# Turning by VectorE in 32 by 32 blocks instead of by TensorE: routed attention followed by a mixture of experts

## The chip, the cores and the metric

The kernel runs on one core of one Trainium2 chip. The metric is the device time of one execution in microseconds (us), here the median of three runs. The core has five engines that run side by side, each with its own queue of instructions, worked off in order: TensorE (PE) multiplies matrices and can also turn (transpose) a tile by multiplying it with an identity matrix; VectorE (DVE) and ScalarE (ACT) work element by element[...], and SyncE (SP) issues transfers. TensorE writes into the small memory PSUM[...]; the large memory on the core is SBUF, with 128 partitions (rows).

## The reference, cut to what matters

Attention among tokens of the same cluster, then a mixture of eight experts in which each token goes to one expert.

```python
# q, k, v: (4 batches, 8 heads, 768 positions, 64 dims); centroids: (8 heads, 16 clusters, 64 dims)
q_assign = np.argmax(np.einsum('bhsd,hcd->bhsc', q_n, c_n), axis=-1)   # nearest centroid of each query
k_assign = np.argmax(np.einsum('bhsd,hcd->bhsc', k_n, c_n), axis=-1)
mask = q_assign[:, :, :, None] == k_assign[:, :, None, :]
scores = scale * np.matmul(q, k.transpose(0, 1, 3, 2))                 # scale = 1 / sqrt(64)
scores = np.where(mask, scores, -1000000000.0)
attn = softmax(scores)                                                 # written out in the reference
x = np.matmul(attn, v)                                                 # to (3072 tokens, 512)
# experts: y = relu(x_e @ w1[e]) @ w2[e] for the tokens of expert e, times the gate's weight
```

## The kernel before

Heads are worked two at a time: a *pair* g is one batch and two heads, and there are NG = 16 pairs. A pair has 12 *score units* (2 halves of the queries by 6 blocks of 128 keys), done in 2 *turns* of 6 units (NB = 6, TG = 2). The even turn 2g does the first half of the queries, the odd turn 2g+1 the second. Once all pairs are done the experts follow, which the change does not touch.

For each pair, q and k come in with the positions in the partitions and must be turned so that the 64 dimensions are there. The similarity to the centroids then comes out with clusters in the partitions, is turned back for the maximum over the clusters, and the one-hot rows are turned once more, because the mask goes into the scores as a second product: a bf16 product of one-hots, with a large constant where clusters differ.

```python
def load_qk(g):                                   # two transfers for q, two for k, by SyncE
    ...
        t = rows[g, name] = ld.tile([P, NQ, 2, D], F32, name=name + "_in")
        for a in range(2):
            nc.sync.dma_start(out=t[:, :, a, :], in_=src[b, 2 * hp + a].rearrange("(p j) d -> p j d", j=NQ))

def turn(g, piece):                               # 12 TensorE transposes a pair, and the copies out of PSUM
    ...
    for i in range(n):
        w, j = divmod(8 * piece + i, NQ)
        nc.tensor.transpose(ps[:, i * P : (i + 1) * P], rows[g, "qk"[w]][:, j].rearrange("p a d -> p (a d)"), ident)
    ...                                           # piece 0: DVE multiplies q by the scale (L777; ACT for pair 1), ACT copies k (L778)
        nc.scalar.copy(flat[:, 1024 : 2 * S], ps[:, 0 : 2 * S - 1024])      # piece 1 (L780)

def similar(g):                                   # q and k times the centroids
    ...
    nc.tensor.matmul(ps[...], lhsT=cblk[...], rhs=qk[g][:, w, half * HS : (half + 1) * HS], ...)
    nc.vector.tensor_copy(sims[g], ps[:, 0:HS])   # L792

def similar2(g):                                  # 3 TensorE transposes, then ACT copies
    ...
    nc.scalar.copy(sims[g], ps[:, 0:HS].rearrange("p (t c) -> p t c", c=C))

def assign(g):                                    # where is the maximum: DVE, DVE, GpSimd
    nc.vector.tensor_reduce(mx, sim, axis=AX, op=ALU.max)
    nc.vector.tensor_tensor(sim, sim, mx..., op=ALU.is_ge)
    nc.gpsimd.tensor_tensor(sim, sim, first_c..., op=ALU.mult)

def assign2(g):                                   # the first maximum, as a one-hot
    nc.vector.tensor_reduce(top, rank, axis=AX, op=ALU.max)
    for w in range(2):
        nc.vector.tensor_tensor(ohs..., v(rank, w), top..., op=ALU.is_equal)

def put(g):                                       # 6 TensorE transposes in bf16, ACT copies, DVE scales
    ...
    nc.scalar.copy(oh[:, 0, :], ps[:, 0:S])
    for a in range(2):
        nc.vector.tensor_scalar(oh[a * D : a * D + C, 1, :], ps[...], scalar1=BIG, scalar2=-BIG, ...)   # L835

def score(u):                                     # one unit: 4 products, exp, and a running sum on DVE
    for a in range(2):
        nc.tensor.matmul(ps[:, a, 0:HS], lhsT=qk[g][r, 1, ks], rhs=qk[g][r, 0, qs], start=True, stop=False)       # L855
    for a in range(2):
        nc.tensor.matmul(ps[:, a, 0:HS], lhsT=ohT[g][r, 1, ks], rhs=ohT[g][r, 0, qs], start=False, stop=True)     # L858
    nc.scalar.activation(A[u], ps[:, :, 0:HS], AF.Exp)                                                            # L860
    ...                                           # unit 1 of a turn: T = A[u-1] + A[u] (L863)
        nc.vector.tensor_tensor(T[g, half], T[g, half], A[u], op=ALU.add)    # units 2 to 5 (L867)

def attend(u): ...                                # exp times v, both heads (L875)
def x_turn(g, half): ...                          # 3 TensorE transposes of the result (L941), DVE divides by the sum
```

The order of all this is set by hand. A turn has four parts: its scores, the jobs of part 0, its attend steps, and the jobs of part 1:

```python
else:                                             # pairs 2 to 15
    at(n - 3, 0, turn, g, 0)                      # n = 2 g: an odd turn
    at(n - 3, 0, turn, g, 1)
    at(n - 3, 1, similar, g)
    at(n - 2, 0, similar2, g)
at(n - 2, 0, assign, g)
at(n - 2, 0, assign2, g)
at(n - 1, 0, put, g)
...
for n in range(-4, NTURN + 5):
    for x in range(n * NB, (n + 1) * NB):
        if 0 <= x < NU:
            score(x)
    for f, a in jobs.get((n, 0), ()):
        f(*a)
    for x in range(n * NB, (n + 1) * NB):
        if 0 <= x < NU:
            attend(x)
    for f, a in jobs.get((n, 1), ()):
        f(*a)
```

Jobs of the same place run in the order of the pairs: in an odd turn the put of pair g-1 stands ahead of the turning of pair g. The tile qk has two buffers, so the turned q and k of pair g take the place of those of pair g-2, whose last scores are those of that same odd turn.

## Time and profile before

| | |
|---|---|
| median of three runs | 777.03 us (776.28 to 777.63) |
| span of the profiled execution | 776.7 us |
| attention (scores begin to the last attend) | about 18 to 404 us |
| PE busy | 755.2 us (97%) |
| DVE busy | 449.8 us (58%) |
| ACT busy | 299.0 us (38%) |
| granted TensorE clock, mean | 0.991 |

In a line of the timeline the columns are the start in us, the length in us, the engine, the line of the kernel and the operation, the tile written and those read, their shapes and how often; in brackets how long the engine had been idle before it and what ended that. A matmul in f32 shows as two instructions. Ends of matmuls are modelled and overlap the next start by a little, so the steps between starts are what counts. A line of a group gives, after the shapes and the count, the total busy time in us and the mean of one in ns, then the idle time ahead. A line of a stretch of time gives, for each engine, busy us and the number of instructions, then the granted clock of TensorE, the share of the DMA engines and GB/s.

### The profile page before, as it was taken

What the parts mean: (1) busy time and instruction counts of PE and PEld (TensorE: products, weight loads), DVE (VectorE), ACT (ScalarE), POOL (GpSimd) and SP (SyncE); (2) the same over time, 40 slices, a digit from 0 to 9 for tenths busy, and PEclk for the clock granted to TensorE, in tenths of its full rate; (3) what the DMA queues carried; (4) which work ended last, traced back from release to release, by engine and by line L of the source; (5) the groups of instructions that cost most, each with busy time, mean ns of one, the idle gap of its engine ahead of it and who ended that gap; (6) DMA issues with size and microseconds to landing.
All of it is one profiled execution on the core that took longest, in us unless ns stands there. A gap on an engine that the chain in (4) does not pass through costs nothing.

```text
span 776.7 us, 12417 instructions
## 1 busy us (share of the span) xinstructions
PE 755.2 (97%) x5021; PEld 485.7 (63%) x5021; DVE 449.8 (58%) x758; ACT 299.0 (38%) x481; POOL 111.0 (14%) x157
## 2 busy tenths in 40 slices
PE   6999999999999999999999999999999999999994
PEld 4544555445554455544556668787888898787861
DVE  3667677666676666778743544555564655555200
ACT  4545645556455564555531112232222214132210
POOL 2200000100000000001200541311312121211101
PEclk9999999999999999999999999999999999999998
DMA  9025501455115221120103446747556675847540
GB/s 221 6 62 204 136 26 37 144 208 131 30 33 144 62 62 31 32 103 1 45 1 135 152 127 224 267 166 253 221 216 219 246 261 178 308 155 246 212 156 18
DMA packets 85281, 106.41 MB, mean 137 GB/s; under 512 B 52831, under 2 KB 56927, under 8 KB 84704
## 3 DMA queue, kind: packets, MB, share of 16 engines
q1 hardware_dynamic: 79616, 85.99, 34.9%
q0 software_dynamic: 4928, 19.51, 6.8%
q8 instruction: 41, 0.67, 0.4%
q14 instruction: 24, 0.20, 0.1%
q10 hardware_dynamic: 672, 0.05, 0.1%
HBM read 92.90 MB, written 13.16 MB: 137 GB/s over the span
## 4 chain that ended last, share of the span: by engine, by line
PE 80%; issue 9%; DVE 6%; POOL 2%; ACT 2%; ACTq 0%; POOLq 0%; DVEq 0%
PE sps L855 15%; PE O L875 13%; PE sps L476 10%; PE sps L310 9%; PE sps L498 8%; PE sps L364 7%; PE sps L858 4%; PE mps L896 3%; DVE T L867 3%; PE sps L787 2%; PE sps L344 2%; PE sps L770 2%; PE sps L291 2%; PE sps L941 1%; PE mps L909 1%
## 5 line engine op out<-in xcount | busy, mean ns | idle before, releaser
L860 ACT ACTIVATE A<-sps 128x768 f32<-128x768 f32 x192 | 153.3, 812 | 53.4 <-PE sps L858 52.3
L855 PE MATMUL sps<-qk 64*128 64x384 f32 x768 | 160.6, 497 | 0.1
L867 DVE TENSOR_TENSOR T<-T,A 128x768 f32<-128x768 f32 x128 | 122.7, 959 | 14.4 <-ACT lsT L902 0.5
L875 PE MATMUL O<-A,v_in 128*64 128x384 f32 x768 | 130.9, 490 | 0.0
L855 PEld LDWEIGHTS sps<-qk 64*128 64x128 f32 x768 | 66.9, 189 | 50.4 <-issue 42.3
L875 PEld LDWEIGHTS O<-A,v_in 128*64 128x64 f32 x768 | 52.2, 137 | 62.6 <-issue 62.5
L858 PE MATMUL sps<-ohT 64*128 64x384 bf16 x384 | 63.6, 325 | 0.0
L364 PE MATMUL sps<-w,h_sb 128*128 128x512 f32 x144 | 63.1, 592 | 0.0
L310 PEld LDWEIGHTS sps<-xgT,w 128*128 128x128 f32 x512 | 58.3, 192 | 4.5 <-issue 2.5
L863 DVE SCALAR_TENSOR_TENSOR T<-A 128x768 f32<-128x768 f32 x32 | 30.7, 958 | 49.1 <-ACT A L860 49.1
L310 PE MATMUL sps<-xgT,w 128*128 128x128 f32 x512 | 58.7, 275 | 0.0
L328 POOL DMA_INDIRECT out_dram<-zo,s_idx x32 | 33.3, 1041 | 154.2 <-ACT zo L324 90.9
L274 POOL DMA_INDIRECT xg<-x_rows,g_idx x32 | 37.7, 1179 | 112.8 <-ACT gate L284 100.9
L808 POOL TENSOR_TENSOR sim<-sim,first_c 128x384 f32<-128x384 f32 x16 | 16.0, 999 | 264.2 <-DVE sim L807 264.2
L364 PEld LDWEIGHTS sps<-w,h_sb 128*128 128x128 f32 x144 | 26.7, 190 | 30.6 <-issue 30.6
L883 ACT COPY xT<-O 128x384 f32<-128x384 f32 x32 | 15.5, 483 | 62.1 <-PE O L875 62.0
L476 PEld LDWEIGHTS sps<-xs,w1s 128*128 128x128 f32 x288 | 36.0, 190 | 4.2 <-DVE xs L387 4.2
L476 PE MATMUL sps<-xs,w1s 128*128 128x144 f32 x288 | 37.8, 288 | 0.0
L324 ACT ACTIVATE zo<-sps,gate 128x512 f32<-128x512 f32 x12 | 8.2, 687 | 72.1 <-PE sps L364 60.1
L858 PEld LDWEIGHTS <-ohT 64*128 64x128 bf16 x384 | 19.5, 95 | 25.3 <-issue 0.6
L297 DVE COPY xgT<-sps 128x512 f32<-128x512 f32 (+1 forms) x20 | 10.8, 566 | 40.6 <-PE sps L291 40.6
L498 PE MATMUL sps<-w2s,hs 128*128 128x256 f32 x144 | 33.6, 383 | 0.0
(246 smaller groups left out, 988.2 us busy)
## 6 DMA issues: line engine op xcount, KB each, us to landing
w<-in_moe_w_dram SPq DMA_DIRECT2D x32, 2048.0 KB, 9.2
x_rows<-x POOLq DMA_DIRECT2D x4, 1548.0 KB, 6.5
q_in<-in_q_dram SPq DMA_DIRECT2D x32, 192.0 KB, 4.4
k_in<-in_k_dram SPq DMA_DIRECT2D x32, 192.0 KB, 4.8
v_in<-in_v_dram SPq DMA_DIRECT2D x16, 384.0 KB, 3.3
xg<-x_rows,g_idx POOLq DMA_INDIRECT x32, 4.5
out_dram<-zo,s_idx POOLq DMA_INDIRECT x32, 5.5
csb<-in_centroids_dram ACTq DMA_DIRECT2D x1, 32.0 KB, 1.9
```

The source lines that it names most:

```text
L274: nc.gpsimd.indirect_dma_start(out=g["xg"][0:m, j, :], out_offset=None, in_=x_d[0 : g["rows"], :], in_offset=bass.IndirectOffsetOnAxis(ap= ...
L310: nc.tensor.matmul(o, lhsT=g["w"][0][:, c, fb * P : (fb + 1) * P], rhs=g["xT"][:, c, :cols], start=(c == 0), stop=(c == DB - 1),)
L328: ins = nc.gpsimd.indirect_dma_start(out=out[:, :], out_offset=bass.IndirectOffsetOnAxis(ap=g["si"](j)[0:m], axis=0), in_=zo[0:m], in_offs ...
L364: nc.tensor.matmul(zp, lhsT=g["h"][:, fb, j * P : (j + 1) * P], rhs=g["w"][1][:, fb, :], start=(fb == 0), stop=(fb == FB - 1),)
L476: nc.tensor.matmul(o, lhsT=a[:, c, f * P : (f + 1) * P], rhs=b[:, c, :], start=(c == 0), stop=(c == KH - 1),)
L498: nc.tensor.matmul(ps[:, 0, 0:DH], lhsT=a[:, f, :], rhs=b[:, f, :], start=(f == 0), stop=(f == FH - 1),)
L855: nc.tensor.matmul(ps[:, a, 0:HS], lhsT=qk[g][r, 1, ks], rhs=qk[g][r, 0, qs], start=True, stop=False)
L858: nc.tensor.matmul(ps[:, a, 0:HS], lhsT=ohT[g][r, 1, ks], rhs=ohT[g][r, 0, qs], start=False, stop=True)
L860: nc.scalar.activation(A[u], ps[:, :, 0:HS], AF.Exp)
L863: nc.vector.scalar_tensor_tensor(T[g, half], in0=A[u - 1], scalar=1e-9 / P, in1=A[u], op0=ALU.add, op1=ALU.add)
L867: nc.vector.tensor_tensor(T[g, half], T[g, half], A[u], op=ALU.add)
L875: nc.tensor.matmul(O[g, half][a * D : (a + 1) * D, 0:HS], lhsT=rows[g, "v"][:, a, j, :], rhs=a_[:, a, :], start=(j == 0), stop=(j == NQ - 1),)
```

## The change

TensorE is relieved of three kinds of turning, which VectorE now does with its own transpose, an instruction that turns every 32 by 32 block by itself:

- q and k of pairs 1 to 15 (`turn_blocks`). As only blocks are turned, the positions and dimensions must come in so arranged that the turned blocks form the wanted layout: the loads are cut into quarters, each 32 of the 128 head-and-dimension rows, in pieces of 32 numbers (128 bytes; 64 numbers before). There is no copy out of PSUM; the scale moves into the exponential.
- the similarities (`similar`): the copy out of PSUM is itself the transpose; `similar2` goes.
- the one-hots (`assign2`): one compare, then one transpose. `put` places the blocks with eight small copies, of which four apply the large constant.

`assign2` moves from the even turn to the odd one. The first pair is still turned by TensorE, in another order, its whole assignment runs on DVE, k of the first pair is loaded through ACT's queue, the squares of the centroids move to DVE, and 23 idle matmuls stand between its similarity and its scores. Cut to its core:

```diff
-                for a in range(2):
-                    nc.sync.dma_start(out=t[:, :, a, :], in_=src[b, 2 * hp + a].rearrange("(p j) d -> p j d", j=NQ))
+                for quad in range(4 if g else 0):
+                    a, d0 = quad // 2, quad % 2 * 32
+                    nc.sync.dma_start(
+                        out=t[quad * 32 : (quad + 1) * 32].rearrange("p j a d -> p (j a d)").rearrange(
+                            "p (i m d) -> p i m d", m=4, d=32
+                        ),
+                        in_=src[b, 2 * hp + a].rearrange("(m p i) d -> p i m d", m=4, i=NQ)[:, :, :, d0 : d0 + 32],
+                    )
+                for a in range(0 if g else 2):
+                    (nc.scalar if g == 0 and name == "k" else nc.sync).dma_start(...)
 ...
-        for i in range(12):
-            nc.tensor.matmul(ps[:, 0:P], lhsT=ident, rhs=ident, start=True, stop=True)
+        idle(ps, 13)
 ...
+        for i in range(2):
+            t = ohp.tile([P, 2, S], BF16, name=f"ohT{i}")
+            nc.gpsimd.memset(t, 0.0)
+        nc.gpsimd.iota(part_i, pattern=[[0, 1]], base=0, channel_multiplier=1)
+        ...                      # six small DVE instructions make big[P, 2, 2] of it
-        nc.scalar.activation(csq, csb, AF.Square, accum_out=cs2)
+        nc.vector.tensor_tensor(csq, csb, csb, op=ALU.mult)
+        nc.vector.reduce_sum(cs2, csq, axis=AX)
 ...
+        def turn_blocks(g):
+            qk[g] = qkp.tile([P, 2, S], F32, name="qk")
+            for w in range(2):
+                nc.vector.transpose(qk[g][:, w, :], rows[g, "qk"[w]].rearrange("p j a d -> p (j a d)"))
 ...
-            sims[g] = asg.tile([P, HS], F32, name="simT", bufs=1)
-            nc.vector.tensor_copy(sims[g], ps[:, 0:HS])
-        def similar2(g): ...
+            sims[g] = asg.tile([P, HS], F32, name="sim")
+            nc.vector.transpose(sims[g], ps[:, 0:HS])
 ...                              # assign2
+            oh = asg.tile([P, HS], BF16, name="oh")
+            nc.vector.tensor_tensor(groups_of(oh), rank, top.unsqueeze(2).to_broadcast([P, G, C]), op=ALU.is_equal)
+            sims[g] = asg.tile([P, HS], BF16, name="ohs")
+            nc.vector.transpose(sims[g], oh)
 ...                              # put
+            for half in range(2):
+                cols = slice(half * HS, (half + 1) * HS)
+                for a in range(2):
+                    ...
+                    nc.vector.tensor_copy(oh[r, 0, cols], t[q])
+                    nc.vector.tensor_scalar(
+                        oh[r, 1, cols], t[k], scalar1=big[k, a, 0:1], scalar2=big[k, a, 1:2], op0=ALU.mult, op1=ALU.add
+                    )
 ...
-            nc.scalar.activation(A[u], ps[:, :, 0:HS], AF.Exp)
+            nc.scalar.activation(A[u], ps[:, :, 0:HS], AF.Exp, scale=D**-0.5)
 ...                              # the order
+                at(-2, 1, idle_of, 23)
+                at(-1, 1, turn_blocks, g)          # pair 1
+                at(0, 0, similar, g)
+                at(0, 1, assign, g)
+                at(1, 0, assign2, g)
+                at(1, 0, put, g)
             else:
-                at(n - 3, 0, turn, g, 0)
-                at(n - 3, 0, turn, g, 1)
+                at(n - 3, 0, turn_blocks, g)
                 at(n - 3, 1, similar, g)
-                at(n - 2, 0, similar2, g)
-            at(n - 2, 0, assign, g)
-            at(n - 2, 0, assign2, g)
-            at(n - 1, 0, put, g)
+                at(n - 2, 0, assign, g)
+                at(n - 1, 0, assign2, g)
+                at(n - 1, 0, put, g)
```

## The prediction

> **What bounds the kernel now.** I read the busy times and slices of the page first, then the timeline of TensorE (PE) and of VectorE (DVE) over one pair of heads in the steady part, then the groups of instructions for durations, and last the granted clock by 2 us stretches at the start.

> ```profile
> PE 755.2 (97%) x5021; PEld 485.7 (63%) x5021; DVE 449.8 (58%) x758; ACT 299.0 (38%) x481; POOL 111.0 (14%) x157
> ```

> PE is busy 97% of the span, so at first sight every PE instruction taken away is time gained. But the share is an average, and the change trades PE work for DVE work at one place of the loop. There are 16 pairs; each is two turns of six score units. I call the first turn of a pair the even turn and the second the odd turn. Work that prepares pair g (turning, similarity) is done in odd turn 2g-3, together with the placing of the one-hots of pair g-1. This is PE in an odd turn of the middle:

> ```profile
> 151.59 0.92 PE L855 MATMUL sps<-qk 64*128 64x384 f32 x4
> ...
> 156.38 0.33 PE L858 MATMUL sps<-ohT 64*128 64x384 bf16 x2
> 156.64 0.51 PE L828 MATMUL sps<-ident_b,oh 128*128 128x128 bf16 x6
> 156.99 0.82 PE L770 MATMUL sps<-ident,q_in 128*128 128x128 f32 x6
> 157.65 0.82 PE L770 MATMUL sps<-ident,k_in 128*128 128x128 f32 x6
> 158.40 4.09 PE L875 MATMUL O<-A,v_in 128*64 128x384 f32 x24
> 162.42 0.55 PE L941 MATMUL sps<-ident,xT 128*128 128x128 f32 x3
> 162.90 0.85 PE L787 MATMUL sps<-qk,cblk 128*32 128x384 f32 x8
> 163.68 0.92 PE L855 MATMUL sps<-qk 64*128 64x384 f32 x4
> ```

> Read from S = 151.59: six scores to S+5.05, transposes to S+6.8, attention times v to S+10.8, the x transposes, the similarity matmuls at S+11.31, and the next turn at S+12.09. No hole. The same turn on DVE:

> ```profile
> 154.36 0.96 DVE L863 SCALAR_TENSOR_TENSOR T<-A 128x768 f32<-128x768 f32 x1 [1.45 <-ACT A L860]
> 155.51 4.15 DVE L867 TENSOR_TENSOR T<-T,A 128x768 f32<-128x768 f32 x4 [0.20 <-ACT A L860]
> 159.68 1.12 DVE L835 TENSOR_SCALAR ohT<-sps 16x768 bf16<-16x768 bf16 x2
> 160.83 0.96 DVE L777 TENSOR_SCALAR qk<-sps 128x768 f32<-128x768 f32 x1
> ```

> The reader is to see that DVE is late, although idle 42% on average: the sum T cannot begin before the second exponential, and its five steps go at 1.04 us each where scores come every 0.81 us. So T ends at 159.66 = S+8.07, about 3 us after the last score. Only then come the one-hots (1.12) and the copy of qk (0.96), to 161.79; ScalarE follows with its part, and the similarity starts at 162.90, just when PE gets there. DVE's tail is nearly critical already. In the odd turn with a gate in it (T ends at 134.5) PE does wait:

> ```profile
> 137.48 0.55 PE L941 MATMUL sps<-ident,xT 128*128 128x128 f32 x3
> 138.56 1.33 PE L787 MATMUL sps<-qk,cblk 128*32 128x384 f32 x8 [0.53 <-ACT qk L778]
> ```

> [...]768 elements take 0.96 us (T) and 384 take 0.55 us (the reduction and the copy below), and I use these. [...]with only transposes and idleness on PE from 10.9 to 16.1 us the granted clock falls, and it is back between 22 and 24:

> ```profile
> 14.00:16.00 2.00, 0.00 (x0) 0.00 (x0) 1.10 (x3) 0.53 (x2) 0.83 (x1) 0.94 1.25 242
> 16.00:18.00 2.00, 1.87 (x14) 0.76 (x14) 0.26 (x2) 0.80 (x1) 0.00 (x0) 0.50 1.25 275
> ...
> 22.00:24.00 2.00, 2.00 (x14) 0.98 (x14) 0.97 (x2) 1.59 (x3) 0.00 (x0) 0.85 0.00 0
> ```

> The 0.50 is the granted clock.

> **Removed from PE, per pair in the steady part.** The chain gives 12 turns of q and k 1.32 us, 6 one-hot transposes 0.44, and 3 similarity transposes 0.48: 2.24 us. The first two lie in the odd turn (1.76), the third in the even turn. If PE stayed the bound, 14 pairs would give 14 x 2.24 = 31 us.

> **Added to DVE in the odd turn.** The order of instructions in the changed kernel is, after the last T: assign2 and put of pair g-1, then the two turns of q and k of pair g. The similarity matmuls of pair g need those turns. The scores, v products and x transposes on PE no longer have anything between them. The old rows that price the new ones:

> ```profile
> L814 DVE TENSOR_REDUCE top<-sim 128x24 f32<-128x384 f32 x16 | 8.8, 553 | 19.0 <-POOL sim L808 19.0
> L792 DVE COPY simT<-sps 128x384 f32<-128x384 f32 x16 | 8.9, 558 | 10.0 <-PE sps L787 9.9
> L867 DVE TENSOR_TENSOR T<-T,A 128x768 f32<-128x768 f32 x128 | 122.7, 959 | 14.4 <-ACT lsT L902 0.5 <-DVE T L863 0.5 <-ACT A L860 0.5
> L835 DVE TENSOR_SCALAR ohT<-sps 16x768 bf16<-16x768 bf16 x32 | 17.8, 555 | 2.3 <-ACT ohT L833 1.7
> ```

> - Maximum (top): 0.55. It was in the even turn and now stands behind T in the odd one.
> - The one-hot, 384 elements: 0.56, as the similar L807 (558 ns). It moves with top.
> - Its transpose, bf16, 384 elements: 0.58.
> - put: 8 small instructions of 32 by 384 in bf16. L835 takes 555 ns; [...]0.25 each, 2.0 together. This is an estimate; 0.15 to 0.35 each is possible.
> - Two turns of 768 elements: 2 x 0.97 = 1.94.
> - Small gaps of 0.03 to 0.04 between dependent ones, as in the trace: 0.15.

> Sum 5.8, against 2.1 in these places before. DVE ends the turns at S+8.07+5.8 = S+13.9; with 0.1 of handing over the similarity starts at S+14.0. PE, with 1.76 less to do, is ready for it at S+11.31-1.76 = S+9.55. So it waits 4.4 us, and the similarity is 2.7 us later than before (14.0-11.31). The even turn loses 0.48 us of PE work and its DVE has room (assign keeps two instructions of 0.55). Net of a pair: +2.7-0.48 = +2.2 us, 23.9 to 26.1.

> ScalarE gets less work (copies of 0.37+0.59+0.80+0.48 us a pair go away), which is off the path. The loads are cut into 128-byte pieces from 256-byte ones, twice the packets; the DMA share between 96 and 193 us is 0.37, loads land in a median of 4.4 to 4.8 us and are issued over a turn (12 us) ahead. Even at twice that they stay hidden.

> **The start.** Before, scores begin at 18.39 us and run at half clock to about 22, which costs some 2 us. Now the centroid square is on DVE behind an index that GpSimd makes only after two memsets of 128x1536 (before: 2 x 128x768 in 1.50, so 3.0 us): ready at some 5.9 instead of 2.9. The norms come out near 9.5 instead of 6.75. Then three fewer hops between engines, but the put of 2.0: I get scores from about 19.0, at full clock thanks to the 23 idle matmuls. The second turn starts at 28.8 (before 29.96), its T ends near 36.9, its tail at 42.7, and the third turn starts near 43.6; before 43.27. So zero to +0.3 for the start and first odd turn together.

> **Sum.** 13 further odd turns x 2.7 = +35; 14 even turns x -0.48 = -6.7; start +0.3: +29 us, that is 806. To that comes the clock: a hole of 4.4 us, 4.9 from the last real matmul, [...]may drop the clock in some odd turns. At the start about 5.5 us went at half speed, so about 2.7 us lost each time. [...]but I doubt that it is that regular, and add 4. Predicted 810.

> **Rivals.** (1) PE stays the bound: -31, 746 us. For it: PE's 97%, and the DVE share of 58% seems to leave room. Against it: the DVE tail is serial behind T and the similarity stands behind it. Even with puts of 0.15 and turns of 0.9 the tail is 4.8 us (0.55+0.56+0.5+1.2+1.8+0.15), still 1.2 us more a pair, +16 us. I don't see how it gets faster; 4 in 100. (2) The same wait with cheap small instructions: 790 to 795, on the border of 2%. (3) The wait with the clock falling in most odd turns, or with f32 transposes at half the rate (+1.7 us a pair): 825 to 850. (4) Late loads: [...]128-byte pieces could land late at pairs 4 to 7 beside the weights. Then only those pairs grow, by some us in all.

> **Range and chances.** The tail is uncertain by about 1 us either way: 13 us on the total; the clock adds only upward. Range 790 to 838. Below 761.5 I give 0.04, between 761.5 and 792.6 0.13, above 0.83.

> **What would show it.** Right: the similarity matmuls in odd turns wait some 4 us with the turn of k on DVE as releaser; pairs take about 26 us; T still ends about S+8; the granted clock has dips in mid-attention if the clock takes part. Wrong: pairs of 22 us without a wait (rival 1, tail or order misread); the turns themselves waiting for DMA (rival 4); transposes far from 0.97 us or puts far from 0.25, which rescales the 2.7.

## The result, and the profile after

| | before | after |
|---|---|---|
| median of four runs | 777.33 us (776.28 to 778.21) | 830.51 us (829.92 to 832.45) |
| ratio after to before | | 1.0689, 95% interval 1.0666 to 1.0712 |
| span of the profiled execution | 776.7 us | 828.2 us |
| last attend ends | 404.2 us | 455.7 us |
| granted TensorE clock, mean | 0.991 | 0.958 |

The changed kernel is 6.9% slower. All of it lies in attention: the last attend ends 51.5 us later, and the spans differ by the same 51.5. The page of the changed kernel, busy times and granted clock:

```profile
PE 753.9 (91%) x4745; PEld 467.7 (56%) x4745; DVE 492.4 (59%) x879; ACT 266.3 (32%) x415; POOL 110.2 (13%) x156
...
PEclk9999999899998999998899999999999999999998
```

PE has 276 instructions less, and is busy for nearly as long; a busy time in us grows when the clock is low (four score products take 1.59 us below, where it has fallen, and 0.92 us in the kernel before at full clock). DVE is busy for 43 us more, and its share is 59%, after 58%: an engine can hold up another one and still look idle.

The waits of PE, in the list of who waited for whom (us in total, times, longest): a new one, of the similarity matmuls for the turning on DVE, 14 times, once for each pair from 2 to 15.

```profile
PE sps L829 <- DVE qk L822: 57.7, 14, 5.1
```

One of the odd turns, on PE (start us, us, instruction) and then on DVE:

```profile
310.51 4.09 PE L912 MATMUL O<-A,v_in 128*64 128x384 f32 x24
314.53 0.55 PE L978 MATMUL sps<-ident,xT 128*128 128x128 f32 x3
318.80 2.35 PE L829 MATMUL sps<-qk,cblk 128*32 128x384 f32 x8 [3.73 <-DVE qk L822]
321.09 1.59 PE L892 MATMUL sps<-qk 64*128 64x384 f32 x4
```

```profile
309.30 4.15 DVE L904 TENSOR_TENSOR T<-T,A 128x768 f32<-128x768 f32 x4
313.36 0.55 DVE L854 TENSOR_REDUCE top<-sim 128x24 f32<-128x384 f32 x1
313.94 0.56 DVE L856 TENSOR_TENSOR oh<-sim,top 128x384 bf16<-128x384 f32 x1
314.53 0.58 DVE L861 STREAM_TRANSPOSE ohs<-oh 128x384 bf16<-128x384 bf16 x1
315.15 0.25 DVE L872 COPY ohT<-ohs 32x384 bf16<-32x384 bf16 x1
315.41 0.37 DVE L873 TENSOR_SCALAR ohT<-ohs,big 32x384 bf16<-32x384 bf16 x1
...
317.77 0.98 DVE L822 STREAM_TRANSPOSE qk<-q_in 128x768 f32<-128x768 f32 x1
318.67 0.94 DVE L822 STREAM_TRANSPOSE qk<-k_in 128x768 f32<-128x768 f32 x1
```

DVE works without a break from the sum T to the turning of k; the first products of the similarity go as soon as q is turned, the others after k. Between the x transposes and the similarity PE stands still for 3.7 us, 4.2 from the end of the attend steps. The similarity then takes 2.35 us where it took 0.85, for two reasons: it waits for k in the middle, and the clock has fallen. The same time in stretches of 1 us (PE busy, then the granted clock, DMA share, GB/s):

```profile
318.00:319.00 1.00, 0.20 (x2) 1.00 0.00 0
319.00:320.00 1.00, 1.00 (x6) 0.54 0.00 0
...
321.00:322.00 1.00, 1.00 (x6) 0.50 0.82 129
322.00:323.00 1.00, 1.00 (x8) 0.75 0.89 140
```

The clock falls to half at about 319.1, after PE has begun again, and is back at about 322.5. Added up over attention as 1 less the granted clock, in stretches of 1 us, there are 14 such falls, one for each of the 14 turns with the hole: ten sum to 1.7 us each, four to 3.4 us, together 30.7 us. The kernel before has one fall, at its start (15.8 to 22.6 us), which sums to 3.4 us.

### The profile page after: what moved, and what is told of

It is laid out like the page before. It is cut to its first block, busy times and chain, and to the rows that moved or that the text cites. A ratio compares the mean times of both kernels' runs of the same rounds, so it can differ in the third digit from the quotient of the medians.

```text
span 828.2 us, 12007 instructions
## 1 busy us (share of the span) xinstructions
PE 753.9 (91%) x4745; PEld 467.7 (56%) x4745; DVE 492.4 (59%) x879; ACT 266.3 (32%) x415; POOL 110.2 (13%) x156
## 4 chain that ended last, share of the span: by engine, by line
PE 72%; DVE 13%; issue 9%; POOL 2%; ACT 1%; DMA 1%; DVEq 0%; POOLq 0%; ACTq 0%
PE sps L892 15%; PE O L912 10%; PE sps L481 9%; PE sps L315 8%; PE sps L503 7%; PE sps L369 7%; PE sps L829 4%; DVE T L904 4%; PE sps L895 3%; PE mps L933 3%; DVE ohT L873 2%; DVE qk L822 2%; PE sps L349 2%; PE sps L296 1%; DVE ohT L872 1%
## 5 line engine op out<-in xcount | busy, mean ns | idle before, releaser
L892 PE MATMUL sps<-qk 64*128 64x384 f32 x768 | 169.9, 522 | 0.9 <-DVE x L981 0.8
L904 DVE TENSOR_TENSOR T<-T,A 128x768 f32<-128x768 f32 x128 | 122.7, 958 | 14.4 <-ACT A L897 1.2
L892 PEld LDWEIGHTS sps<-qk 64*128 64x128 f32 x768 | 70.5, 200 | 61.2 <-issue 53.6
L829 PE MATMUL sps<-qk,cblk 128*32 128x384 f32 x128 | 35.1, 775 | 58.0 <-DVE qk L822 57.7
L920 ACT COPY xT<-O 128x384 f32<-128x384 f32 x32 | 15.4, 480 | 101.0 <-PE O L912 101.0
L829 PEld LDWEIGHTS sps<-qk,cblk 128*32 128x32 f32 x128 | 5.6, 132 | 72.3 <-DVE qk L822 71.1
L302 DVE COPY xgT<-sps 128x512 f32<-128x512 f32 (+1 forms) x20 | 10.8, 566 | 40.6 <-PE sps L296 40.6
```

The costliest lines, as they stand in the source:

```text
L829: nc.tensor.matmul(ps[t * 2 * C : (t + 1) * 2 * C, 0:HS], lhsT=cblk[:, g % HP].rearrange("p a c -> p (a c)"), rhs=qk[g][:, w, half * HS : ...
```

## The experiments

The theory: DVE's tail behind T holds up the similarity, and the hole on PE lets the clock fall. Rivals: the 128-byte loads; the block turning as such; DVE's total work, whatever its place; the clock harmless or low for another reason. A *pair* below is the step from one pair's similarity to the next, read at the scores that follow it (before: 23.87 us, 24.9 to 25.3 in gate turns, the odd turns, one in four pairs, in which the experts' gate is also worked out for a batch). The *hole* is the time from the end of the attend steps to the similarity; PE does 0.5 us of x transposes in it.

**e1: keep PE warm in the hole.**

```diff
                 at(n - 3, 0, turn_blocks, g)
+                at(n - 3, 1, idle_of, 18)
                 at(n - 3, 1, similar, g)
```

> The changed kernel with 18 idle matmuls in each odd turn, between the x transposes and the similarity, where PE waits 4.2 to 5.5 us for DVE. Theory (DVE's tail behind T, and on top a clock that falls in the hole it leaves): the wait itself stays, the granted clock stays at 1.0, and the similarity and the first scores of the next turn run at full rate. In the odd turn at 262 us the stretch from the similarity to the third score takes 5.5 us and would take about 2.9; 14 times 2.6 is 36, so 795 us (788 to 802). Rival (the low clock costs nothing because DVE sets the pace of the even turn too, or it comes from something other than the hole): 825 to 831.

Measured: 809.46 us, 1.0419 times the kernel before (1.0398 to 1.0439); clock 0.997, no fall in attention. Pairs take 26.27 us, where the changed kernel has 27.3 to 28.5. PE in an odd turn of this run:

```profile
274.60 4.18 PE L728 MATMUL mps<-ident 128*128 128x128 f32 x36
278.71 1.48 PE L829 MATMUL sps<-qk,cblk 128*32 128x384 f32 x8
280.12 0.92 PE L892 MATMUL sps<-qk 64*128 64x384 f32 x4
```

The idle matmuls fill the hole, and the scores are at full rate at once. So 21.0 us of the 53.2 are the clock (830.51 - 809.46), and the falls come from the hole; some 32 us are left for waiting less what the start wins. I had expected 795: the similarity is 1.48 us long even at full clock, because k is turned in its middle, and of the 30.7 us that the falls take from PE only 21.0 lengthen the run. The rest, as I read it, only replaces waiting (the similarity takes 2.35 us at half clock and 1.48 at full, so it does not double).

**e2: assign2 back in the even turn.**

```diff
-                at(n - 1, 0, assign2, g)
+                at(n - 2, 0, assign2, g)
                 at(n - 1, 0, put, g)
```

> The changed kernel with assign2 (maximum, compare and one-hot transpose on DVE, 1.7 us) back in the even turn, as in the kernel before. Theory: DVE's tail behind T shrinks by 1.7 us, the hole on PE from 4.2 to 2.5 us[...]. Odd turn about 13.3 us, even 11.3: a pair of 24.6, in all about 785 us (778 to 795). If only the wait matters and the clock does not: 830 - 14 x 1.7 = 806. If assign2's place does not matter (the loads or the turning of q and k are the cause): 828 to 831.

Measured: 804.09 us, 1.0352 (1.033 to 1.0373). Neither number came: the hole shrank from 4.2 to 2.2 us as worked out, but the clock, which the 785 took to stay up, still fell, in 2 of 9 ordinary turns and in four with a longer hole (the first, the last, two with a gate), 15.4 us in all. Pairs without a fall take 25.06 us, not 24.6: assign2 now delays DVE's x product, and scores wait for the PSUM tile that it frees (10 waits, 5.3 us in total).

**e11: the same, kept warm,** on top of e2.

```diff
+                at(n - 3, 1, idle_of, 10)        # on top of e2
```

> The changed kernel with assign2 in the even turn and 10 idle matmuls in the hole of each odd turn (2.2 us, 3.5 in gate turns). Theory: the clock does not fall any more; its six falls there took 15 us of full-speed time in all, of which some two thirds counted, so 804 becomes 794 (790 to 798), and an undisturbed pair stays at 25.1 us. If the falls are free in that kernel: 803.

Measured: 793.16 us, 1.0208 (1.0191 to 1.0225), no fall, pairs of 25.05 us. As expected: the six falls cost 10.9 us. With e1 this gives the price of assign2's place without the clock: 809.46 - 793.16 = 16.3 us, or 1.2 us a pair for 1.7 us of DVE work.

**e3: put in the even turn too.**

```diff
-                at(n - 1, 0, assign2, g)
-                at(n - 1, 0, put, g)
+                at(n - 2, 0, assign2, g)
+                at(n - 2, 1, put, g)
```

> The changed kernel with assign2 in the even turn and put at its end, so that in the odd turn only the two turns of q and k (1.9 us) stand behind T. Theory: the hole on PE nearly goes, but DVE carries put into the start of the odd turn, T starts about 2 us later there and ends at about S+9.6 instead of S+8.1; a pair of about 23.9 us, in all 770 to 782 us. If T is not delayed (the small instructions fit in DVE's idle time): 22.4 us a pair, 750 to 758. Rival (loads, or the turning itself): 825 or more.

Measured: 787.22 us, 1.0139 (1.0116 to 1.0162). Ordinary pairs take 23.95 us, as worked out, with a hole of 1.1 us and no fall. The total is 5 us above the range: the first odd turn keeps the old order, gate turns take 25.4 to 26.4 us, and three falls (first, last and one gate turn) cost something more. Of the 53 us, 43 go away with the same work on the same engines, so the loads and the turning itself, both unchanged here, can account for at most the other 10; e9 below takes those away too.

**e4: q and k turned by PE again.**

```diff
-                at(n - 3, 0, turn_blocks, g)
+                at(n - 3, 0, turn, g, 0)         # 12 transposes on PE; DVE copies 512 of q's 768 columns
+                at(n - 3, 0, turn, g, 1)
```

> The changed kernel with q and k of all pairs turned by PE again and loaded in the old pieces; similarities and one-hots stay on DVE in 32 by 32 blocks. Theory: the tail behind T is still assign2 1.7 + put 2.6 + the copy of q 0.7 = 5.0 us, PE gets 1.3 us of work back, so the hole is about 2.2 us and the clock stays: a pair of about 25.2, in all 795 us (787 to 803). Rival (the 128-byte loads and the block turning of q and k are what costs): the loss goes wholly, 765 to 777.

Measured: 816.34 us, 1.0509 (1.0479 to 1.0539). The wait for DVE is there without any block turning of q and k: the similarity starts 5.17 us after T ends (5.0 worked out), the hole is 2.55 us. What I had wrong is the clock: it falls in 11 of 14 turns. So taking q and k off DVE helps by only 14 us, and with 256-byte loads and PE's own turning this kernel is still 39 us behind the kernel before.

**e5: the loads alone.** The kernel before, with the quarter loads added:

```diff
+                if g:
+                    x_ = ld.tile([P, NQ, 2, D], F32, name="qk_x", bufs=1)   # read by nothing
+                    for quad in range(4): ...                               # the changed kernel's transfers, for q and for k
```

> The kernel before, which in addition loads q and k of pairs 1 to 15 a second time in the changed kernel's quarters (32 by 24 by 32 numbers, 128-byte pieces) into a tile that nothing reads. Theory (the loads lie beside other work): 775 to 779 us, as before. Rival (128-byte pieces hold up transfers that something waits for): 785 or more.

Measured: 777.23 us, 0.9994 (0.9985 to 1.0002), with 179362 DMA packets in place of 85281. The loads lie beside other work.

**e8: the start alone.** The start of the changed kernel, and pairs 1 to 15 as before:

```diff
+                at(n - 3, 1, similar_o, g)       # _o: the functions of the kernel before
+                at(n - 2, 0, similar2_o, g)      # and so on; turn copies q in two pieces, scale in the exponential
```

> Only the start of the changed kernel: pair 0 assigned on DVE, k of pair 0 by ACT's queue, the squares on DVE, the 23 idle matmuls; pairs 1 to 15 are turned and assigned by PE, ACT and DVE as in the kernel before (the scale stays in the exponential). Theory: 1.5 to 2.5 us less than before, about 775 us (773 to 776.5). If the start is worth nothing: 777.

Measured: 771.65 us, 0.9927 (0.9911 to 0.9944), more than expected. The third turn begins at 41.1 us instead of 43.3, which is the start's 2.2 us. The other 3.7 us are not the start: here DVE copies 512 columns of q and not 768, and the gate turns lose their wait (23.86 us in place of 24.9 to 25.3). That fits a tail behind T that was just critical in the kernel before, as the prediction read it; the shorter copy was not tried alone.

**e6: PE turns q and k, ACT alone copies them.**

```diff
+                    nc.scalar.copy(qk[g][:, :, 0:512], ps.rearrange("p (w s) -> p w s", w=2))   # in place of DVE's copy
-                at(n - 3, 0, turn_blocks, g)
+                at(n - 3, 0, turn, g, 0)
+                at(n - 3, 0, turn, g, 1)
-                at(n - 1, 0, assign2, g)
+                at(n - 2, 1, assign2, g)         # behind the x product
```

> Similarities and one-hots on DVE as in the changed kernel; q and k of all pairs turned by PE, but copied out of PSUM by ACT alone; assign2 at the end of the even turn, behind the work that the x transposes wait for; put in the odd turn. Only put (2.6 us) stands behind T, and nothing on PE but the next scores waits for it. Theory: no hole on PE longer than half a us outside the gate turns, no fall of the clock, PE saves 0.48 + 0.44 us a pair against the kernel before: 22.95 us a pair, start 1.5 to 2 us earlier, 762 us (756 to 770). Rival (DVE's total work, not its place, is the bound; it is only some 1 us a pair less than in the changed kernel): 800 or more.

Measured: 765.03 us, 0.9847 (0.983 to 0.9863); pairs of 23.09 us (22.95 worked out), hole 0.4 us, one fall, late. That is 1.5% under the kernel before. Some 6 us of it are what e8 wins as well; beyond that, pairs take 23.09 us where e8 has 23.86. So similarities and one-hots on DVE are a gain once nothing but put stands behind T.

**e7: everything on DVE, in another order, four copies on ACT.**

```diff
                 at(n - 3, 0, turn_blocks, g)
+                at(n - 3, 1, put_late, g - 1)    # the four scaling copies, behind the x product
                 at(n - 3, 1, similar, g)
-                at(n - 1, 0, assign2, g)
-                at(n - 1, 0, put, g)
+                at(n - 2, 1, assign2, g)
+                at(n - 1, 0, put_q, g)           # the four plain copies, now on ACT
```

> The changed kernel's whole work, in another order and with the four plain copies of put on ACT: assign2 at the end of the even turn, the two turns of q and k first behind T, then the x product, the four scaling copies of put, then the similarity's transpose. Theory: the turns end about S+10.4, the hole on PE is under 1 us, the scaling copies are done shortly before the next scores need them: 22.6 to 23.2 us a pair, 755 to 768 us, clock 0.99. Rival (DVE is the bound by its sum, the same instructions but four): 795 or more. Between: T starts late because DVE is still at assign2, and scores wait for the PSUM tile that the x product frees: 770 to 780.

Measured: 762.41 us, 0.9811 (0.9795 to 0.9827); ordinary pairs of 22.45 us, slightly under the range worked out. The total is in its range, and neither the rival nor the case between came.

**e9: the order alone.** As e7, but with all eight instructions of put on DVE in `put_late`, so that every engine has exactly the changed kernel's instructions:

```diff
                 at(n - 3, 0, turn_blocks, g)
+                at(n - 3, 1, put_late, g - 1)
                 at(n - 3, 1, similar, g)
-                at(n - 1, 0, assign2, g)
-                at(n - 1, 0, put, g)
+                at(n - 2, 1, assign2, g)
```

> The changed kernel with its own instructions, all on the same engines, in another order only: assign2 at the end of the even turn, then in the odd turn behind T first the two turns of q and k, the x product, all eight instructions of put, the similarity's transpose. Theory (the order, not the sum of work, costs the time): the hole before the similarity goes as in the run with ACT copying; put ends 1.0 us later than there, so the first scores of the next turn wait for one-hots and for the PSUM tile that the similarity's transpose frees, about 1 us: 23.4 us a pair, 770 to 782 us. Rival (it was ACT taking over four copies that won the time): 800 or more.

Measured: 774.62 us, 0.997 (0.9958 to 0.9983); pairs of 23.4 us, clock 0.994. DVE and then PE in an odd turn of this run:

```profile
203.21 0.97 DVE L822 STREAM_TRANSPOSE qk<-q_in 128x768 f32<-128x768 f32 x1
204.10 0.94 DVE L822 STREAM_TRANSPOSE qk<-k_in 128x768 f32<-128x768 f32 x1
...
207.64 0.38 DVE L873 TENSOR_SCALAR ohT<-ohs,big 32x384 bf16<-32x384 bf16 x1
208.05 0.58 DVE L836 STREAM_TRANSPOSE sim<-sps 128x384 f32<-128x384 f32 x1
```

```profile
204.04 0.55 PE L978 MATMUL sps<-ident,xT 128*128 128x128 f32 x3
204.52 1.42 PE L829 MATMUL sps<-qk,cblk 128*32 128x384 f32 x8
205.86 0.92 PE L892 MATMUL sps<-qk 64*128 64x384 f32 x4
...
208.69 0.92 PE L892 MATMUL sps<-qk 64*128 64x384 f32 x4 [0.80 <-DVE sim L836]
```

The similarity follows the x transposes at once, as q and k are the first thing that DVE does behind T. put goes on until 208.0, beside scores, and what is left is a wait of 0.8 us for the PSUM tile that the similarity's transpose frees. The changed kernel's 879 DVE instructions and 4745 of PE take 55.9 us less in this order. This decides against DVE's total work as the bound, and against ACT's share as the reason of e7 (12 of its 68 us).

**e10: the same order for pair 1 as well,** on top of e7:

```diff
-                at(1, 0, assign2, g)
-                at(1, 0, put, g)
+                at(0, 1, assign2, g)
+                at(1, 0, put_q, g)               # and put_late at (1, 1)
```

> The kernel of the run with another order and ACT copying, with the same order for pair 1 as well, whose odd turn still has the old tail there (hole 4.2 us, one fall of the clock of 3.4 us). Theory: 3 to 4 us less than its 762.4, so 757 to 760. If the start hides it: 762.

Measured: 757.69 us, 0.9748 (0.9732 to 0.9764). The hole at the first odd turn goes from 4.2 to 0.7 us, its fall with it. This is the best version: 2.5% under the kernel before, with the idea of the change kept whole (0.7% is what e8 wins without it).

## Why the prediction was right, point by point

It said 810 us, 790 to 838, slower by over 2%. 830.51 is in the range and 20 us above the point. The wait was worked out rightly; that the total stayed inside the range is owed to its wide upper end, as the clock was mis-sized. By its steps:

- **The place of the wait** was right: the similarity in odd turns waits for DVE's turning of q and k, 14 times, with DVE as releaser (q first, then k).
- **T at S+8.07** held: in the odd turn that begins at 247.88 us, T ends at 255.86, S+7.98.
- **The tail of 5.8 us** measured 6.16 (313.45 to 319.61). Its terms: maximum 0.55 (0.54 mean), compare 0.56 (0.558), one-hot transpose 0.58 (0.578), two turns 1.94 (1.84 from start to end). The prices of the transposes and of put's instructions were the prediction's estimates, as no trace before the change has such instructions. The mis-sized one is put: 2.0 was assumed at 0.25 for each of eight; the four copies take 0.25, but the four with a scalar per partition take 0.373, and put lasts 2.6 us.
- **The standstill of 4.4 us** (4.9 from the last real matmul) was 3.7 (4.2): the similarity starts 5.36 us after T, when q is turned, and not 5.9. But it then waits for k and is 1.48 us long in e1, not 0.85. The two errors nearly cancel, which is luck: by the prediction's terms the next scores begin at S+14.8, and in e1 they begin at S+14.97 (265.15 to 280.12).
- **+2.2 us a pair without the clock** was +2.40 (e1: 26.27 against 23.87), and +29 us in all was some +32.
- **The start, zero to +0.3 us,** was -1.45 us at the third turn, and -2.1 with PE warm (41.18 against 43.27). Scores begin at 16.34 us and not at 19.0, at full clock (1.00 in each stretch from 14 to 24 us): the two memsets of GpSimd (POOL) took 2.69 us and not 3.0, norms were done at 8.7 and not 9.5, and the first scores do not wait for put (15.32 to 17.97 us): they follow directly on the idle matmuls, which end at 16.41.
- **The clock, +4 us,** is the step that failed in size: 21.0 us. The 4 was judgement: the prediction doubted that the falls come regularly. But of the 14 holes of 4.2 us and more, all brought a fall, and in e2 and e4 part of the holes of 2.2 to 2.6 us did so too. In the windows of 3.413 us of the last section PE need not be idle throughout: one with 1.65 us of work was followed by a fall (e2). Wherever a standstill of 3.7 us lies, one of the windows that it touches has at most 3.41 - 3.73 / 2 = 1.55 us of work. This is an estimate from those traces. Each fall cost some 1.5 us, not 2.7.
- **The rivals:** PE as the bound (746 us) was out; late loads were out (e5, and the 30 turns of q and k on DVE stand idle for 0.5 us in all before they start); cheap small instructions were out (put took 2.6 us). Rival 3, the wait with the clock falling in most odd turns, is what happened, at its lower end.
- "I don't see how it gets faster" was right for this order alone: e9 has the same instructions and is 0.3% faster than the kernel before. The prediction took the order as given and did not say how much of the loss hung on it.

## What to carry to other kernels

Before work moves from the busiest engine to an idler one, look at when the idler one is idle: DVE had 42% free, but only some 1 us of it between T and the similarity (159.66 to 162.90 us before, with 2.1 us of work in it), where the new work was put. Order a queue by who waits for each result: the same instructions cost 830 us with the two that PE waits for at the end of the row behind T, and 775 us with them at its head and assign2 moved out of it. A hole on PE of a few us can cost more than itself, since the clock falls after it (some 1.5 us each here, 21 in all); idle matmuls in the hole tell in one run how much.

## What the runs showed of the hardware

```profile
89.55:92.96 3.41, 1.65 (x11) 1.00 0.38 115
92.96:96.37 3.41, 3.41 (x14) 0.50 0.77 121
...
301.17:304.59 3.42, 1.75 (x10) 1.00 0.49 134
304.59:308.00 3.41, 3.41 (x26) 1.00 0.83 131
```

- Over the thirteen traces, from 22 us on, half clock followed all 39 windows at full clock in which PE was busy for less than 1.4 us, 3 of 12 with 1.5 to 1.7 us, and none of the other 2784. In the changed kernel alone it followed all 15 with 0.84 us or less, and none of the other 201, where PE was busy for 2.25 us or more. In attention and at the start, half clock ended after one window where PE was busy in it for 3.07 us or more (from 39.19 us in the changed kernel), and stayed for a second with 3.04 us or less: 3.04 at the start of the kernel before, 1.85 to 1.99 in the gate turns of the changed kernel. So a fall can come after PE has begun again (319.08 us, after 318.80). The time in which PE is busy is the profile's; what the chip itself counts is not shown.
